# Retention and two MLPs on one core: scores as 64 by 64 products, and chunk loads into buffers that come free

## The chip, the cores and the metric

The kernel runs on one core of a Trainium2 chip. The metric is device time in microseconds (us), one launch, lower is better. TensorE (PE) multiplies and writes PSUM; its weight loads are listed apart as PEld. VectorE (DVE), ScalarE (ACT) and GpSimd (POOL) work on the products, and the queue of SyncE (SP) issues every DMA. An engine carries out its instructions in the order of the program and waits at semaphores for the others.

## The reference

```python
# retention: B=2, H=8 heads, S=768 steps, D=64
state = gamma * state + k_t (outer) v_t        # per head
y_t   = scale * q_t @ state
x = y transposed to (1536 tokens, 512)
h = x @ moe_w_in;  g = h * tanh(softplus(h));  x = g @ moe_w_out     # 512 -> 2048 -> 512
h = x @ moe2_w_in; g = h * cos(h);             out = g @ moe2_w_out
```

The weights arrive in 64-bit floats. Inputs of the large products are split into a high and a low part, and three products (high-high, high-low, low-high) are summed.

## The kernel before

The recurrence is done in chunks of 128 steps: 12 chunks, numbers 0 to 5 for the first batch entry and 6 to 11 for the second. A chunk's data (q and k transposed, v, k) are 1 MB and come by two DMAs of 512 KB (`att_load`, L281): the first half is q and k transposed ("qk"), the second v and k ("vk"). For each chunk n, TensorE does four groups of products, in this text called by their lines:

- **scores n** (L325, tile `ps_s`): for each of four pairs of heads and each head of the pair, k times q, contraction over D=64. One head's k and q lie in partitions 0 to 63, the other's in 64 to 127. The output of one product is 128 keys by 128 queries.
- **inter n** (L370, `ps_y<-qd,st`): decayed q times the state carried from chunk n-1; 64 by 64 weights. Not for chunks 0 and 6, which begin a batch entry.
- **update n** (L341, `ps_u`): k times decayed v, added to the running state. Not for chunks 5 and 11.
- **out n** (L381, `ps_y<-p,qkv`): masked scores times v.

TensorE's order is scores n+1, inter n, update n, out n, scores n+2, and so on. Beside it, DVE masks the scores (`p`, L332), ACT or POOL makes decayed v (`vd`, L305/L308), POOL makes decayed q (`qd`, L313 to L316), ACT or DVE reads the state out of PSUM (`st`, L350/L353), and ACT and DVE split the output into high and low parts (`x`, L395 and L398). After out 11 the first product of the MLPs starts (`ps_h`, L428), and from there on TensorE works on `ps_h` and `ps_o` (L451) to the end.

The order on each engine comes from a planner (`Plan`, L72): every operation is entered with a cost in us, what it needs and which buffers it takes, and a list schedule by longest remaining path then gives each engine's order. The orders of PE and of SP's first loads are given by the order of entry.

Ten of the twelve chunks have a buffer of their own: 0 and 1 in the third x tile, 2 to 4 in a pool of three, 5 to 7 in the buffers of the output weights (`wo`), 8 and 9 in those of `g`; 10 and 11 reuse the buffers of 2 and 3. So the first twenty chunk loads wait for no buffer. Each load does wait until the load eight before it has landed. SP issues the loads in this order: constants, chunks 0 to 6, the first half of the first input weights (`raw`, L211), chunks 7 to 9, the second half of these weights, chunks 10 and 11, the two halves of the next input weights.

## Time and profile before

| What | Value |
|---|---|
| Median of 3 runs | 572.69 us (571.97 to 572.76) |
| Profiled execution | 573.28 us |
| Its span on the core | 571.5 us |
| Outside the span | 1.78 us |
| PE busy in the span | 565.8 us (99%) |
| DVE, ACT, POOL busy | 382.6, 230.1, 97.5 us |
| First `ps_h` product starts | 45.7 us into the span |
| Granted PE clock, all windows | 1.00 |

The span is the time from the first to the last instruction of the core. A busy PE counts matmuls from issue to their modelled end, so consecutive ones overlap; start-to-start distances tell more than durations. One matmul of 32-bit floats stands as two records in the trace.

### The profile page before, as it was taken

How to read it: one execution, taken by the hardware profiler on the slowest of the kernel's cores; microseconds unless marked ns; L12 is line 12 of the kernel's file. 1: busy time of each engine (PE TensorE's matmuls, PEld its weight loads, DVE VectorE, ACT ScalarE, POOL GpSimd, SP SyncE). 2: the span in 40 equal slices, each digit the busy share in tenths (PEclk: the TensorE clock that was granted, in tenths of full speed). 3: DMA queues.
4: the chain of work that ended last, by engine and by line, in shares of the span. 5: the costliest groups of instructions: out<-in, count | busy, mean ns of one | idle time of the engine just before them, and what ended most of it. 6: DMA issues, size and time to landing. Idle time of an engine off the chain costs nothing.

```text
span 571.5 us, 7260 instructions
## 1 busy us (share of the span) xinstructions
PE 565.8 (99%) x3054; PEld 468.4 (82%) x3054; DVE 382.6 (67%) x416; ACT 230.1 (40%) x284; POOL 97.5 (17%) x74
## 2 busy tenths in 40 slices
PE   8999999999999999999999999999999999999997
PEld 6888888888888888888888888888888888888886
DVE  5779889662375427653487985898498894765462
ACT  3574543422303303214326465465345354354240
POOL 6680001111110301111101111032010312010000
PEclk9999999999999999999999999999999999999999
DMA  8982254422032200412021030304004010000113
GB/s 297 413 335 75 75 210 158 147 75 73 1 131 91 73 1 0 148 73 75 0 75 73 26 123 1 138 10 147 1 0 148 32 41 2 1 1 1 73 38 110
DMA packets 14721, 49.91 MB, mean 87 GB/s; under 512 B 1632, under 2 KB 2016, under 8 KB 14688
## 3 DMA queue, kind: packets, MB, share of 16 engines
q1 hardware_dynamic: 14688, 49.44, 23.4%
q8 instruction: 24, 0.39, 0.3%
q14 instruction: 9, 0.07, 0.0%
HBM read 46.29 MB, written 3.15 MB: 86 GB/s over the span
## 4 chain that ended last, share of the span: by engine, by line
PE 94%; DMA 4%; SPq 1%; ACT 0%; issue 0%; DVE 0%; ACTq 0%
PE ps_h L428 46%; PE ps_o L451 46%; DMA qkv<-qkv_dram 4%; SPq L294 1%; PE ps_y L381 1%; PE ps_y L370 1%; PE ps_s L325 1%; PE ps_u L341 0%; ACT vd L308 0%; ACT x L395 0%; DVE acc L517 0%; SPq L758 0%; ACT st L353 0%; ACTq L308 0%
## 5 line engine op out<-in xcount | busy, mean ns | idle before, releaser
L428 PE MATMUL ps_h<-x,wi 128*128 128x512 f32 x1152 | 264.8, 389 | 0.0
L428 PEld LDWEIGHTS ps_h<-x,wi 128*128 128x128 f32 x1152 | 216.1, 188 | 45.0 <-issue 0.2
L451 PE MATMUL ps_o<-wo,g 128*128 128x512 f32 (+1 forms) x588 | 132.5, 385 | 0.0
L451 PE MATMUL ps_o<-g,wo 128*128 128x512 f32 x576 | 132.3, 389 | 0.0
L451 PEld LDWEIGHTS ps_o<-wo,g 128*128 128x128 f32 x588 | 108.9, 188 | 22.1
L451 PEld LDWEIGHTS ps_o<-g,wo 128*128 128x128 f32 x576 | 108.1, 188 | 22.5
L494 DVE TENSOR_TENSOR g<-mish,g 128x1024 fp32r<-128x1024 f32 x24 | 33.4, 1393 | 59.2 <-ACT g L490 59.2
L262 POOL TENSOR_TENSOR wo<-mag,wo 128x1024 fp32r<-128x1024 f32 x14 | 35.8, 2557 | 212.8 <-ACT wo L248 212.8
L510 DVE TENSOR_TENSOR acc<-ps_o,acc 128x1024 f32<-128x1024 f32 x35 | 42.8, 1222 | 34.6 <-PE ps_o L451 34.4
L262 POOL TENSOR_TENSOR wi<-mag,wi 128x1024 fp32r<-128x1024 f32 x12 | 30.3, 2525 | 193.1 <-ACT wi L248 193.1
L461 ACT ACTIVATE mish<-ps_h 128x1024 f32<-128x1024 f32 (+1 forms) x25 | 24.9, 995 | 95.1 <-PE ps_h L428 95.1
L474 DVE SCALAR_TENSOR_TENSOR turns<-whole,turns 128x1024 f32<-128x1024 f32 x24 | 29.4, 1223 | 44.7 <-ACT whole L470 44.7
L466 ACT ACTIVATE turns<-ps_h,quarter 128x1024 f32<-128x1024 f32 x24 | 26.7, 1114 | 65.4 <-PE ps_h L428 65.1
L239 DVE SCALAR_TENSOR_TENSOR mag<-raw,mag 128x1024 uint32<-128x1024 uint32 (+1 forms) x38 | 42.2, 1110 | 1.1
L483 ACT ACTIVATE turns<-turns 128x1024 f32<-128x1024 f32 x24 | 25.5, 1062 | 34.8 <-DVE turns L480 34.6
L494 DVE TENSOR_TENSOR g<-turns,g 128x1024 fp32r<-128x1024 f32 x24 | 33.2, 1384 | 8.0 <-ACT g L490 8.0
L486 DVE TENSOR_TENSOR turns<-turns,ps_h 128x1024 f32<-128x1024 f32 x24 | 29.2, 1216 | 10.1 <-ACT turns L483 6.8
L254 DVE SCALAR_TENSOR_TENSOR mag<-raw,mag 128x1024 uint32<-128x1024 uint32 x26 | 33.7, 1301 | 0.4
L490 ACT CAST g<-turns 128x1024 fp32r<-128x1024 f32 x24 | 25.1, 1044 | 16.9 <-DVE turns L486 16.9
L248 ACT CAST wi<-mag 128x1024 fp32r<-128x1024 f32 (+1 forms) x20 | 17.5, 876 | 27.3 <-DVE mag L254 22.4
L470 ACT ACTIVATE whole<-turns,magic 128x1024 f32<-128x1024 f32 x24 | 27.7, 1153 | 0.8
L480 DVE TENSOR_SCALAR turns<-turns 128x1024 f32<-128x1024 f32 x24 | 27.0, 1126 | 0.8
(50 smaller groups left out, 330.2 us busy)
## 6 DMA issues: line engine op xcount, KB each, us to landing
qkv<-qkv_dram SPq DMA_DIRECT2D x24, 512.0 KB, 10.1
raw<-w1i_dram SPq DMA_DIRECT2D x16, 512.0 KB, 4.2
raw<-w1o_dram SPq DMA_DIRECT2D x16, 512.0 KB, 4.1
raw<-w2i_dram SPq DMA_DIRECT2D x16, 512.0 KB, 4.0
raw<-w2o_dram SPq DMA_DIRECT2D x16, 512.0 KB, 3.6
out_dram<-acc SPq DMA_DIRECT2D x11, 256.0 KB, 2.1
out_dram<-acc SPq DMA_DIRECT2D x2, 128.0 KB, 1.7
few<-consts_dram SPq DMA_DIRECT2D x1, 146.0 KB, 2.2
```

Source lines behind the costliest of these rows:

```text
L239: nc.vector.scalar_tensor_tensor(out=a, in0=high, scalar=0xC0000000, in1=a, op0=ALU.bitwise_and, op1=ALU.bitwise_or)
L254: nc.vector.scalar_tensor_tensor(out=w_all_of(it, single)[:, ns], in0=raw_t[it][:, ns, :, 0], scalar=29, in1=mag_t[it][:, ns], op0=ALU.log ...
L262: eng.tensor_sub(out=w[:, :, 1], in0=w_all_of(it, single)[:, ns].bitcast(F32), in1=w[:, :, 0].bitcast(F32))
L428: nc.tensor.matmul(h[:, 0 if h_tag(k) == "s" else f % 2, :], w[:, f % 2, a, kk * 128 : (kk + 1) * 128], x[:, b, kk, :], start=(a + b + kk ...
L451: nc.tensor.matmul(ps, lhs, rhs, start=(n == 0), stop=(n == 3 * GF - 1))
L466: nc.scalar.activation(out=t_t[k], in_=h_t[k], func=AF.Identity, scale=INV_2PI, bias=quarter)
L470: nc.scalar.activation(out=n_t[k], in_=t_t[k], func=AF.Identity, bias=magic)
L474: nc.vector.scalar_tensor_tensor(out=t, in0=n_t[k], scalar=MAGIC, in1=t, op0=ALU.subtract, op1=ALU.subtract)
L480: nc.vector.tensor_scalar(out=t, in0=t, scalar1=-0.5, scalar2=0.5, op0=ALU.max, op1=ALU.min)
L486: nc.vector.tensor_mul(out=t_t[k], in0=t_t[k], in1=h_t[k])
L494: nc.vector.tensor_sub(out=g[:, :, 1, :], in0=t_t[k], in1=g[:, :, 0, :].bitcast(F32))
L510: nc.vector.tensor_add(out=acc, in0=o_t[m * NG + G, j, p], in1=acc)
```

## The change

Scores: the 128 keys of a product are cut in two. Each group has 16 products of 64 keys by 128 queries where it had 8 of 128 by 128; for one pair of heads the four products use the four combinations of upper and lower partitions in and out. The results lie where they lay.

Buffers: a table `HOME` names one of eight places for each chunk. Chunks 5 and 6 are loaded over 0 and 1, chunks 7, 8, 9 over 2, 3, 4, chunk 11 over 7, and chunk 10 goes into one `wo` buffer. Each half has its own entry in the planner. A load into a used place waits for the last reader of that half of the earlier chunk. Chunks 10 and 11 are now entered ahead of the second half of the first weights. Two costs in the planner change.

```diff
-IN_WO = (5, 6, 7)
-IN_G = (8, 9)
+HOME = ("x0", "x1", "a0", "a1", "a2", "x0", "x1", "a0", "a1", "a2", "wo", "a0")
...
     def att_load(g, lo, hi, eng=nc.sync):
...
+        home = HOME[g]
...
+            elif home not in homes:
+                homes[home] = att_p.tile([128, 2048], F32, tag=home, name="qkv", bufs=1)
+            att[g] = homes[home]
         eng.dma_start(out=att[g][:, lo:hi], in_=qkv[g, :, lo:hi])
...
         for a in range(NPAIR):
-            for e in range(2):
-                h = slice(D * e, D * e + D)
-                nc.tensor.matmul(ss[e][:, a, :], qk[h, a, 1, :], qk[h, a, 0, :], start=True, stop=True)
+            for t in range(2):
+                keys = slice(D * t, D * t + D)
+                for e in range(2):
+                    h = slice(D * e, D * e + D)
+                    nc.tensor.matmul(
+                        ss[e][keys, a, :], qk[h, a, 1, keys], qk[h, a, 0, :], start=True, stop=True, skip_group_check=True,
+                    )
...
-        at["s", g] = op("PE", 1.05, att_scores, g, needs=at["qk", g] + [first], new=(s[1], 3, "s"), uses=[chunk(g), s[0]])
+        at["s", g] = op("PE", 0.94, att_scores, g, needs=at["qk", g] + [first], new=(s[1], 3, "s"), uses=[*chunk(g, "qk"), s[0]])
...
-            op("PE", 0.62, att_inter, g, needs=[at["st", g - 1], at["qd", g]], uses=uses, new=(("y", g), 1, y_tag(g)))
+            op("PE", 0.55, att_inter, g, needs=[at["st", g - 1], at["qd", g]], uses=uses, new=(("y", g), 1, y_tag(g)))
...
-    weight(("i", 0, 0), lambda: [chunk_loads(g, cuts) for g in (7, 8, 9)])
-    for g in (10, 11):
-        chunk_loads(g, cuts)
+    weight(("i", 0, 0), lambda: [chunk_loads(g, cuts) for g in (7, 8, 9, 10, 11)])
     weight(("i", 0, 1))
```

On PE, around the scores of chunk 1, the rows before (a row stands for so many products of one kind, with the output's shape):

```order
L787 MATMUL ps_w<-zero 128x256
L325 MATMUL ps_s<-qkv 128x128 x8
L341 MATMUL ps_u<-vd,qkv 64x64 x8
L381 MATMUL ps_y<-p,qkv 64x128 x8
L325 MATMUL ps_s<-qkv 128x128 x8
L370 MATMUL ps_y<-qd,st 64x128 x8
```

and now:

```order
L791 MATMUL ps_w<-zero 128x256
L327 MATMUL ps_s<-qkv 64x128 x16
L345 MATMUL ps_u<-vd,qkv 64x64 x8
L385 MATMUL ps_y<-p,qkv 64x128 x8
L327 MATMUL ps_s<-qkv 64x128 x16
L374 MATMUL ps_y<-qd,st 64x128 x8
```

The order of the groups on PE stays; the scores have twice as many products of half the output.

On SP, the loads from chunk 4's second half on, before, with the semaphores that each waits for (DMAHW is a DMA that landed; one row is one DMA of 512 KB):

```order
L294 DMA qkv<-qkv_dram 128x1024 [waits DMAHW2_49]
L294 DMA qkv<-qkv_dram 128x1024 [waits DMAHW3_49]
L294 DMA qkv<-qkv_dram 128x1024 [waits DMAHW4_49]
L294 DMA qkv<-qkv_dram 128x1024 [waits DMAHW5_49]
L294 DMA qkv<-qkv_dram 128x1024 [waits DMAHW6_49]
L211 DMA raw<-w1i_dram 128x1024 [waits DMAHW7_49]
L294 DMA qkv<-qkv_dram 128x1024 [waits DMAHW0_49]
L294 DMA qkv<-qkv_dram 128x1024 [waits DMAHW1_49]
L294 DMA qkv<-qkv_dram 128x1024 [waits DMAHW2_49]
L294 DMA qkv<-qkv_dram 128x1024 [waits DMAHW3_49]
```

and now:

```order
L294 DMA qkv<-qkv_dram 128x1024 [waits DMAHW2_49]
L294 DMA qkv<-qkv_dram 128x1024 [waits DMAHW3_49,PE_49]
L294 DMA qkv<-qkv_dram 128x1024 [waits DMAHW4_49,PE_49,Pool_49]
L294 DMA qkv<-qkv_dram 128x1024 [waits DMAHW5_49,Pool_49]
L294 DMA qkv<-qkv_dram 128x1024 [waits DMAHW6_49,PE_49,Activation_49]
L210 DMA raw<-w1i_dram 128x1024 [waits DMAHW7_49]
L294 DMA qkv<-qkv_dram 128x1024 [waits DMAHW0_49,Pool_49]
L294 DMA qkv<-qkv_dram 128x1024 [waits DMAHW1_49,PE_49,Activation_49]
L294 DMA qkv<-qkv_dram 128x1024 [waits DMAHW2_49,Pool_49]
L294 DMA qkv<-qkv_dram 128x1024 [waits DMAHW3_49,PE_49,Pool_49]
```

The same loads stand in the same order here; those of chunks 5 to 8 now also wait for engines that read the chunk whose place they take.

On ACT, around the decayed v of chunk 7 (`vd_499`), before. `x_467<-ps_y_474` is the high part of chunk 5's output, `st_550` the state after chunk 6, `st_603` that after chunk 7:

```order
L216 ACTIVATE mag_471<-raw_405 128x512
L308 ACTIVATE vd_499<-qkv_418,cst_92 128x64 x4
L395 CAST x_467<-ps_y_474 128x2x2x128
L308 ACTIVATE vd_499<-qkv_418,cst_92 128x64 x4
L353 ACTIVATE st_550<-ps_u_520,cst_92 128x64 x4
L395 CAST x_467<-ps_y_540 128x2x2x128
L353 ACTIVATE st_603<-ps_u_520,cst_92 128x64 x4
```

and now (`vd_573` is chunk 7's decayed v, `x_522<-ps_y_526` chunk 5's output, `st_599` the state after chunk 6):

```order
L215 ACTIVATE mag_524<-raw_463 128x512
L399 CAST x_522<-ps_y_526 128x2x2x128
L308 ACTIVATE vd_573<-qkv_188,cst_92 128x64 x4
L357 ACTIVATE st_599<-ps_u_578,cst_92 128x64 x4
L308 ACTIVATE vd_573<-qkv_188,cst_92 128x64 x4
L399 CAST x_522<-ps_y_590 128x2x2x128
L357 ACTIVATE st_666<-ps_u_578,cst_92 128x64 x4
```

The state after chunk 6 moves ahead of the second half of chunk 7's decayed v, and chunk 5's output ahead of both halves. POOL's order does not change.

## Rows read from the trace of the kernel before

**Rows 1.** The page: span; instruction queue (fetches, MB, share); chain by engine.
```profile
span 571.5 us, 7260 instructions
...
q8 instruction: 24, 0.39, 0.3%
...
PE 94%; DMA 4%; SPq 1%; ACT 0%; issue 0%; DVE 0%; ACTq 0%
```
**Rows 2.** Chain that ended last, 17 to 79 us: start us, us, what.
```profile
17.44 11.76 DMA qkv<-qkv_dram
...
29.28 0.61 ACT vd L308 x3
...
30.81 0.97 ACT vd L308 x4
...
32.07 0.99 PE ps_y L370 x16
33.06 0.62 PE ps_u L341 x16
...
45.72 32.89 PE ps_h L428 x144
```
**Rows 3.** Timeline of PE, 18.3 to 22.1 us: start us, busy us, work.
```profile
18.82 1.16 PE L325 MATMUL ps_s<-qkv 64*128 64x128 f32 x16
19.91 0.67 PE L370 MATMUL ps_y<-qd,st 64*64 64x128 f32 x16
20.51 0.69 PE L341 MATMUL ps_u<-vd,qkv 128*64 128x64 f32 x16
21.03 1.04 PE L381 MATMUL ps_y<-p,qkv 128*64 128x128 f32 x16
22.00 0.38 PE L325 MATMUL ps_s<-qkv 64*128 64x128 f32 x2
```
**Rows 4.** Line L325, its matmuls: ns min/median/max, first and last start us.
```profile
L325 PE MATMUL ps_s<-qkv x192: 272/272/373, 6.2 to 41.7; 64*128 64x128 f32 x192
```
**Rows 5.** Timeline of SP's queue, 0 to 50 us: chunk loads and weights.
```profile
16.19 8.24 SPq L294 DMA_DIRECT2D qkv<-qkv_dram  x6
25.38 0.33 SPq L211 DMA_DIRECT2D raw<-w1i_dram  x1
```
**Rows 6.** The load issued at 16.19 us (chunk 7, qk), line L294.
```profile
DMA to landing us min/median/max: 11.7/11.7/11.7
```
**Rows 7.** The load issued at 18.70 us (chunk 8, qk), line L294.
```profile
DMA to landing us min/median/max: 11.8/11.8/11.8
```
**Rows 8.** Stretches: us, busy of engines, PE clock, DMA share, GB/s.
```profile
12.40:25.20 12.80, 12.74 (x258) 10.88 (x258) 8.62 (x15) 8.42 (x31) 9.70 (x13) 1.00 1.03 415
```
**Rows 9.** Timeline of PE, 27.5 to 34 us: scores 7 and 8.
```profile
28.05 1.16 PE L325 MATMUL ps_s<-qkv 64*128 64x128 f32 x16
...
30.63 1.16 PE L325 MATMUL ps_s<-qkv 64*128 64x128 f32 x16
```
**Rows 10.** Timeline of ACT, 25 to 33 us: state after chunk 6.
```profile
31.68 0.90 ACT L353 ACTIVATE st<-ps_u,cst 128x64 f32<-128x64 f32 x4
```
**Rows 11.** Timeline of POOL, 25 to 46 us: first and last decayed q.
```profile
30.62 0.73 POOL L313 TENSOR_TENSOR qd<-qkv,cst 128x256 f32<-128x256 f32 x1 [0.18 <-DMA qkv<-qkv_dram]
31.43 1.89 POOL L316 TENSOR_TENSOR qd<-qkv,cst 64x256 f32<-64x256 f32 x2
...
41.15 1.59 POOL L316 TENSOR_TENSOR qd<-qkv,cst 64x256 f32<-64x256 f32 x2
```
**Rows 12.** Timeline, all engines, 38 to 48 us: first weights' second half; inter 11.
```profile
39.05 0.74 ACT L216 ACTIVATE mag<-raw 128x512 f32<-128x512 f32 x1
...
44.03 0.67 PE L370 MATMUL ps_y<-qd,st 64*64 64x128 f32 x16
...
45.75 0.69 DVE L239 SCALAR_TENSOR_TENSOR mag<-raw,mag 128x512 uint32<-128x512 uint32 x1
...
46.62 0.62 ACT L248 CAST wi<-mag 128x512 fp32r<-128x512 f32 x1
```

## The prediction

> **What bounds the kernel now.** First the page: the chain that ended last is TensorE for 94% and DMA for 4% [rows 1]. Then the chain in order of time: a chunk load of 17.44 us that lands at 29.20, ACT's decayed v of chunk 7 at 29.28 and its second half at 30.81, inter 7 at 32.07, and from there TensorE alone, with the first MLP product at 45.72 [rows 2]. Behind that point the chain holds no wait: all that the change can give is an earlier start of the MLPs, if their weights are ready too. So two stretches count: up to inter 7, where a load and ACT decide, and from inter 7 to 45.72, where TensorE's own groups do.

> Third, the timeline of TensorE in a chunk that waits for nothing [rows 3]: start to start scores take 1.09 us, inter 0.60, update 0.52, out 0.97, in all 3.18. To split these: a group's busy time less one matmul (272 ns, the median of scores [rows 4], which I take for all three) is the time from its first start to its last. Scores: 1.16 - 0.27 = 0.89, 16 records. Inter: 0.67 - 0.27 = 0.40, also 16. Out: 1.04 - 0.27 = 0.77. Inter's four tiles of 64 by 64 thus carry more than twice the records per us. I read out and scores as 8 rounds of two records, 0.77/7 = 0.11 us a round, and inter as 4 rounds of four, 0.40/3 = 0.13 with a longer first round. From the last start to the next group's first one it is 1.09 - 0.89 = 0.20 behind scores, 0.20 behind inter, 0.20 behind out; each time the tile shape changes.

> **The change part by part.**

> Scores. 16 products give 32 records, four at a time 8 rounds. First to last start: 7 rounds of 0.11 and a first one that is 0.07 longer, as in inter (0.40 - 2 x 0.11 = 0.18), 0.84. The step to inter keeps the tile shape, so I take one round, 0.11, for it: 0.95 against 1.09, -0.14. Inter then finds its shape set; without the long first round it takes 0.55, -0.05. Together -0.19 a chunk. Bounds: with rounds of 0.133 and a step of 0.20 still paid, 7 x 0.133 + 0.20 = 1.13, a loss of 0.04; with no long first round anywhere, 0.77 + 0.11 = 0.88 and inter 0.53, a gain of 0.28.
> [...]

> Chunks 1 to 6. Here the gain has cover: scores 7 started at 28.05 [rows 9], just as the first half of chunk 7 landed (issued 16.19, 11.7 us: 27.9 [rows 5, 6]). TensorE gets there more than a microsecond earlier and waits. Cost and gain: nothing.

> Loads. Each has 512 KB; at 415 GB/s [rows 8] that is 1.26 us, and the DMA share of 1.03 in that stretch says that the engines are full. With some nine loads' worth of time between issue and landing (11.7/1.26), a load that is issued up to some microseconds later lands in the same place of the queue, as long as the queue does not run dry. The new waits delay issues by little: chunk 5's vk half waits for out 0, chunk 6's for out 1, chunk 7's for out 2 (which before ended about 18.8, right ahead of scores 4 [rows 3], and now about 18.4, against an issue at 17.44 [rows 2]). Behind a waiting load SP holds all later ones, weights too, but five or more loads are still under way at that time. So I leave the landings of chunks 7 to 9 where they were. Chunks 10 and 11 move up by one load, since the weights' half that stood ahead of them at 25.38 [rows 5] goes behind them; nobody waited for them.

> Inter 7. Chunk 8's qk half lands at 18.70 + 11.8 = 30.5 [rows 7], and POOL and scores 8 both start then, at 30.62 and 30.63 [rows 9, 11]. That stays. Scores 8 at 30.55, inter 7 possible at 31.5. Its state: ACT's first half of the decayed v starts at 29.28 and is four pieces, as the second, which took 0.97 [rows 2]; to 30.3, then at once the state, 0.90 [rows 10], to 31.2; before, chunk 5's output and the second half stood ahead of it. So inter 7 goes at 31.5 and takes 0.55, where it began at 32.07 and spread over 0.99, being fed by the state's four parts [rows 2]. Update 7 could start at 32.05; the second half of decayed v now ends at 31.2 + 0.97 = 32.2 and holds its last quarter, about 0.1. Against 33.06 [rows 2]: -0.9.

> From there three times scores and inter follow (9 to 11): 3 x -0.19 = -0.57. Sum: -1.45.

> What is late next. POOL works from 30.62 to 41.15 + 1.59 = 42.74 with hardly a gap [rows 11], and its last piece feeds inter 11. It starts at a landing that I keep, so it ends at 42.5 to 42.7. Inter 11 would start at 44.03 [rows 12] - 1.45 = 42.6. The two meet; I take 0.1 for it. Gain 1.35, and POOL alone allows at most 44.03 - 42.6 = 1.4 unless chunk 8 lands earlier.

> Weights. The second half of the first weights goes behind four chunk loads, 4 x 1.26 = 5.0 us later: at the worst latency seen above, 25.38 + 11.8 + 5.0 = 42.2. Then ACT's magnitude 0.74 [rows 12], at most four short DVE operations of up to 0.69, and the cast of 0.62: 46.3. The product that needs it comes 12 matmuls into the MLPs, 12 x 32.89/144 = 2.74 [rows 2], at 44.4 + 2.74 = 47.1. 0.8 us to spare; cost 0.

> Sum: span 571.5 - 1.35 = 570.15; profiled execution 573.28 - 1.35 = 571.9. The median of the runs lies 0.6 below the profiled one, 572.69, so 571.3.

> **The rivals.**

> Chunks 7 and 8 land earlier. The loads land 11.7 us behind their issue though each is worth 1.26 us of transfer; if a shorter queue takes part of that lag away, TensorE runs by its own groups from chunk 4 on: from 18.82, scores 5 to 8 follow at 3.18 - 0.19 each, less the inter and update that the batch boundary lacks (0.55 and 0.52 once each): 18.82 - 0.4 + 4 x 2.99 - 1.07 = 29.3 for scores 8 in place of 30.55. That is 1.25 more: gain 2.6, 570.1. For it: DMA decides at this place. Against: the share is 1.03 either way, and a full queue in order lands the same load at the same time, however many wait behind it.

> Loads land later. If latency from issue stays, chunk 7's vk half, issued 1.0 later, lands 1.0 later: 30.2; then 0.97 and 0.90 on ACT and the hand-over, inter 7 at 32.2, update 7 at 32.9, gain 0.1 + 0.57: 572.0. More instructions are fetched as well: 12 x 16 records more, each with its weight load, 384 on 7,260 whose fetches are 24 of 0.39 MB/24 = 16 KB [rows 1]; 1.3 fetches more, each 16 KB/(415/16 GB/s) = 0.63 us of one of 16 DMA engines, 0.8 us. With all of that as lag on top it is 572.8. For it: every transfer needs all sixteen engines. Against: the queue is deep.
> [...]

> Slower: scores run two at a time. If the 64 by 64 products of one head and the two key halves don't overlap, there are 16 rounds: 1.09 + 8 x 0.11 = 1.97, +0.88 for each of 11 groups from scores 1 on. They follow one another on TensorE, so nearly all of it comes through, less some 1.5 of waits: +8, 581. It turns slower than before at about 1.2 us a group. For it: nothing. Against: inter's 16 records in 0.40 us with the same four tiles.

> **How the numbers follow.** Forecast 0.50; loads earlier 0.18; loads later 0.25; two at a time 0.04; the rest 0.03 (MLP weights late, over 1 us dearer). The forecast's own range is 1.0 to 1.7 us of gain, by POOL's end and the bounds on a chunk. About 0.2% (1.15 us) is what a measurement tells from no change. Faster: two thirds of the forecast, and the loads-earlier case, 0.51. Same: the other third and most of the late case, 0.37. Slower: 0.12. The range 570.0 to 572.9 holds the forecast, the late case and most of the early one.

> **What would show it.** Scores at 0.95 us start to start and inter at 0.55; scores 8 still at about 30.5, right at its landing; the state after chunk 6 between the halves of decayed v, update 7 near 32.1; POOL without a gap up to about 42.6; the first MLP product at 44.3 and no wait behind it. Wrong: landings of chunks 7 and 8 moved by over half a microsecond either way, a scores group at 1.1 or more, or a gap of TensorE in the first products.

## The result and the profile after

The changed kernel takes 577.49 us (median of 4 runs, 576.51 to 578.70); the kernel before, beside it on the same chip, 572.40 (4 runs, 571.97 to 572.76). The ratio is 1.009, 95% interval 1.0065 to 1.0116. The forecast was 571.3 us, range 570.0 to 572.9: wrong, and on the wrong side.

The page of after first: span, instruction queue, chain by engine.

```profile
span 574.8 us, 7648 instructions
...
q8 instruction: 25, 0.41, 0.3%
...
PE 96%; DMA 2%; issue 1%; SPq 0%; DVE 0%
```

Beside [rows 1] the span is 3.3 us longer, DMA has lost half of its share of the chain, and "issue" has come up: time in which an engine waited for nothing that the profile shows. It is 1% of the span, and more than the whole 3.3 us. The chain in order of time (start us, us, what) has it in four pieces:

```profile
19.79 0.43 PE ps_u L345 x9
20.23 0.79 issue
21.02 0.39 PE ps_u L345 x6
...
25.30 0.81 PE ps_s L327 x23
26.11 1.10 issue
27.22 0.54 PE ps_s L327 x9
...
31.74 0.80 PE ps_s L327 x20
32.54 1.44 issue
33.98 0.55 PE ps_s L327 x10
...
42.49 1.03 PE ps_s L327 x31
43.51 1.44 issue
44.96 0.27 PE ps_s L327
...
48.98 1.13 PE ps_h L432 x4
```

Each time TensorE stops in the middle of a group: update 3 behind 9 of its 16 records, scores 6 behind 23 of 32, scores 8 behind 20, scores 11 behind 31. In these four groups the waits for semaphores, on data or buffers, stand at the first two weight loads; the records behind the stops carry none, and the trace names no releaser for the idle time ahead of them. The four stops make 0.79 + 1.10 + 1.44 + 1.44 = 4.77 us of idle time. Start to start they cost more, because a stop also hides behind the modelled end of the matmul ahead of it: by PE's timeline the four stopped groups take 1.06, 1.34, 1.67 and 1.74 us longer than the same groups elsewhere, 5.8 in all. The first MLP product starts at 48.98, where it was 45.72 [rows 2].

Between the stops the groups run as forecast. PE's timeline of chunk 2 to 3 in after (start us, busy us, work), which answers to [rows 3]:

```profile
15.29 1.10 PE L327 MATMUL ps_s<-qkv 64*64 64x128 f32 x32
16.21 0.62 PE L374 MATMUL ps_y<-qd,st 64*64 64x128 f32 x16
16.76 0.69 PE L345 MATMUL ps_u<-vd,qkv 128*64 128x64 f32 x16
17.28 1.04 PE L385 MATMUL ps_y<-p,qkv 128*64 128x128 f32 x16
18.25 1.10 PE L327 MATMUL ps_s<-qkv 64*64 64x128 f32 x32
```

Start to start scores take 0.92 us, inter 0.55, update 0.52, out 0.97: 2.96 a chunk for 3.18. Those 80 matmul records come with 80 weight loads, 160 instructions a chunk; before it was 128.

Where the stops lie: all of TensorE's records, matmuls, weight loads and its semaphore instructions, are counted from the first one. The records that start behind the stops are the 705th, 961st, 1217th and 1729th; between them lie 256, 256 and 512. The instruction queue's fetches, by the page, are 0.41 MB/25 = 16 KB each, which is 64 bytes for each of 256 records; 25 times 256 is 6,400, and the page counts 6,492 matmuls and weight loads. So the stops are read here as the places where one fetched block ends and the next begins; one such boundary, at 1473, was passed without a stop. The DMA's rows of after for 24.7 to 25.9 us, just ahead of the second stop (packets, MB, share of 16 engines), show a fetch among the loads:

```profile
q1 hardware_dynamic: 131, 0.48, 98.3%
q8 instruction: 1, 0.02, 5.4%
```

### The profile page after: what moved, and what is told of

Its sections match the earlier page's. It is cut to its first block, busy times and chain, and to the rows that moved or that the text cites. A ratio compares the mean times of both kernels' runs of the same rounds, so it can differ in the third digit from the quotient of the medians.

```text
span 574.8 us, 7648 instructions
## 1 busy us (share of the span) xinstructions
PE 564.1 (98%) x3246; PEld 467.6 (81%) x3246; DVE 383.1 (67%) x416; ACT 230.3 (40%) x284; POOL 97.1 (17%) x74
## 4 chain that ended last, share of the span: by engine, by line
PE 96%; DMA 2%; issue 1%; SPq 0%; DVE 0%
PE ps_h L432 45%; PE ps_o L455 45%; PE ps_s L327 2%; PE ps_y L385 2%; DMA qkv<-qkv_dram 2%; PE ps_u L345 1%; PE ps_y L374 1%; SPq L294 0%; DVE acc L521 0%; SPq L762 0%
## 5 line engine op out<-in xcount | busy, mean ns | idle before, releaser
L514 DVE TENSOR_TENSOR acc<-ps_o,acc 128x1024 f32<-128x1024 f32 x35 | 42.7, 1221 | 34.6 <-PE ps_o L455 34.4
L261 POOL TENSOR_TENSOR wi<-mag,wi 128x1024 fp32r<-128x1024 f32 x12 | 30.3, 2527 | 192.9 <-ACT wi L247 167.2
L478 DVE SCALAR_TENSOR_TENSOR turns<-whole,turns 128x1024 f32<-128x1024 f32 x24 | 29.3, 1222 | 44.8 <-ACT whole L474 44.8
L238 DVE SCALAR_TENSOR_TENSOR mag<-raw,mag 128x1024 uint32<-128x1024 uint32 (+1 forms) x38 | 40.7, 1070 | 1.1
L490 DVE TENSOR_TENSOR turns<-turns,ps_h 128x1024 f32<-128x1024 f32 x24 | 29.1, 1214 | 10.1 <-ACT turns L487 6.8
L232 DVE TENSOR_SCALAR mag<-mag 128x1024 uint32<-128x1024 uint32 (+1 forms) x38 | 27.5, 723 | 1.1
```

The lines of the kernel that those rows point to most:

```text
L232: nc.vector.tensor_scalar(out=a, in0=a, scalar1=3, scalar2=0x3FFFFFF8, op0=ALU.logical_shift_left, op1=ALU.bitwise_and)
L238: nc.vector.scalar_tensor_tensor(out=a, in0=high, scalar=0xC0000000, in1=a, op0=ALU.bitwise_and, op1=ALU.bitwise_or)
L261: eng.tensor_sub(out=w[:, :, 1], in0=w_all_of(it, single)[:, ns].bitcast(F32), in1=w[:, :, 0].bitcast(F32))
L478: nc.vector.scalar_tensor_tensor(out=t, in0=n_t[k], scalar=MAGIC, in1=t, op0=ALU.subtract, op1=ALU.subtract)
L490: nc.vector.tensor_mul(out=t_t[k], in0=t_t[k], in1=h_t[k])
L514: nc.vector.tensor_add(out=acc, in0=o_t[m * NG + G, j, p], in1=acc)
```

## The experiments

**New scores alone**, in the buffers of before (e1), and **new buffers alone**, with the scores and costs of before (e2).

The edit of e1, against before:

```diff
-            for e in range(2):
-                h = slice(D * e, D * e + D)
-                nc.tensor.matmul(ss[e][:, a, :], qk[h, a, 1, :], qk[h, a, 0, :], start=True, stop=True)
+            for t in range(2):
+                keys = slice(D * t, D * t + D)
...
+                        ss[e][keys, a, :], qk[h, a, 1, keys], qk[h, a, 0, :], start=True, stop=True, skip_group_check=True,
...
```

The edit of e2, against after:

```diff
...
-                        ss[e][keys, a, :], qk[h, a, 1, keys], qk[h, a, 0, :], start=True, stop=True, skip_group_check=True,
...
+                nc.tensor.matmul(ss[e][:, a, :], qk[h, a, 1, :], qk[h, a, 0, :], start=True, stop=True)
...
```

> The kernel before with the 64 by 64 scores alone (and their two planner costs); buffers and order of loads as before. Theory F (fetches): TensorE runs out of instructions. The trace of the changed kernel has four gaps inside groups, 0.8 to 1.4 us, about 250 or 500 matmul and weight-load records apart, each about 1.3 us behind the end of a 16 KB instruction fetch; scores of twice the products bring 160 instead of 128 instructions a chunk. F expects gaps of the same kind here, three to five of them, 0.5 us or more each, and 574 to 577 us. Theory W (waits): the new buffer waits hold up loads and these cost the time; W expects no such gaps and 570.5 to 571.5.

> The changed kernel with the old scores (8 products of 128 by 128 and the two old planner costs); the loads go into freed buffers as changed. F: 128 instructions a chunk, a block of 256 lasts 6.4 us on TensorE, longer than the 6.1 to 6.7 us or as long as a fetch takes while loads run: no gap over 0.5 us inside a group, 571 to 573. W: the waits are all there, 575 to 578.

e1 took 577.63 us, ratio 1.0088 (1.0072 to 1.0105): all of the loss, and 0.6 us over F's range. Its PE timeline where the idle time ahead is "issue" (in brackets at the end):

```profile
21.37 0.39 PE L345 MATMUL ps_u<-vd,qkv 128*64 128x64 f32 x6 [0.79 <-issue]
27.84 0.54 PE L327 MATMUL ps_s<-qkv 64*64 64x128 f32 x9 [1.38 <-issue]
34.88 0.55 PE L327 MATMUL ps_s<-qkv 64*64 64x128 f32 x10 [1.71 <-issue]
41.07 1.09 PE L385 MATMUL ps_y<-p,qkv 128*64 128x128 f32 x15 [1.42 <-issue]
```

The first three stops come behind the same records as in after, and the boundary that after passed now has one, while after's last has none. e2 took 573.34, ratio 1.0016 (1.0006 to 1.0025), 0.3 us over F's range and well under W's. What its TensorE waited for from 12 to 46 us (us in total, times, longest us) has no "issue":

```profile
PE ps_s L325 <- DMA qkv<-qkv_dram: 0.8, 1, 0.8
PE ps_y L370 <- DVE st L350: 0.2, 1, 0.2
```

The scores make the stops; W falls.

**Loads of half the size** (e3): after, each chunk by four DMAs of 256 KB.

```diff
-    cuts = (0, 1024, 2048)
+    cuts = (0, 512, 1024, 1536, 2048)
```

> The changed kernel with each chunk loaded by four DMAs of 256 KB instead of two of 512 KB; at most eight are under way, so half as many bytes stand in the queues ahead of an instruction fetch. F: a fetch waits less for its turn (before it 3.8 us from request to its packet under load, 1.5 to 1.7 without), the gaps shrink to under 0.5 us in all or vanish, 570.5 to 573. W: the same waits for the same buffers, 576 to 578. Theory S (supply): TensorE's sequencer can't take 160 instructions in 3 us whatever the loads do: gaps as in the changed kernel, 577.

578.93 us, ratio 1.0106 (1.0085 to 1.0127), with five stops (0.65, 1.38, 0.61, 2.24, 0.54 us). F's expectation failed: they did not shrink. With seven or eight loads under way in either kernel, half the bytes were under way, and the packet came no sooner (3.2 to 4.5 us behind the start of a block, in after 3.2 to 4.4 at the four stops).

**No late loads** (e4): after without the loads of chunks 7 to 11, which compute on what lies in the places of chunks 2 to 4.

```diff
+        if g >= 7:
+            att[g] = homes[f"a{(g - 7) % 3}"]
+            return
         home = HOME[g]
```

> The changed kernel without the ten DMAs of chunks 7 to 11; these chunks compute on the data of chunks 2 to 4 that lie in the same kind of buffer (this leaves out part of the work, so its time is no version's). Instructions and their order on all engines but SP are those of the changed kernel. F: from about 22 us on, no loads stand ahead of a fetch; the gaps at 26 to 45 us vanish, the one at 20 us may stay; 569.5 to 572. S: the gaps stay, 575 or more. W: no waits for those buffers any more either, 569.5 to 572, so this run tells F and W from S, not from one another.

573.86 us, ratio 1.0021 (1.0012 to 1.0031), 1.9 us over F's and W's range and under S's. Its PE timeline has two stops and then none:

```profile
21.41 0.39 PE L348 MATMUL ps_u<-vd,qkv 128*64 128x64 f32 x6 [1.73 <-issue]
...
27.61 0.54 PE L330 MATMUL ps_s<-qkv 64*64 64x128 f32 x9 [1.10 <-issue]
```

The windows of e4 (us, busy of PE, PEld, DVE, ACT, POOL, PE clock, DMA share, GB/s), while loads run and when they have ended:

```profile
12.40:25.20 12.80, 11.06 (x286) 9.48 (x280) 7.70 (x14) 6.75 (x25) 10.05 (x14) 1.00 1.03 415
28.00:41.00 13.00, 13.00 (x345) 11.28 (x338) 10.12 (x17) 9.76 (x37) 9.49 (x12) 1.00 0.02 6
```

At a DMA share of 0.02, TensorE is busy for 13.00 of 13.00 us with the same 64 by 64 products: S falls. The second stop, which F expected to vanish, stayed: the weights' loads had moved up into the free queue, and the DMA share was still 1.04 from 25 to 26 us, when the fetch's packet came at 25.18. That stop is a part of the time over the range.

**Where the blocks end** (e9): after, with 16 more warm-up products of zeros ahead of scores 1.

```diff
-    op("PE", 1.1, zeros, 10, "u")
+    op("PE", 2.86, zeros, 26, "u")
```

> After with 16 more products of zeros (26 for 10) between scores 0 and scores 1, where TensorE waits for a load anyway; 16 products with their weight loads are 32 instructions. Theory F (the stops lie at the ends of 256-instruction blocks): every stop moves 16 matmul records earlier in the program. In after they come behind 9 of 16 records of update 3, 23 of 32 of scores 6, 20 of 32 of scores 8, 31 of 32 of scores 11; now behind 9 of 16 records of inter 3, 7 of 32 of scores 6, 4 of 32 of scores 8, 15 of 32 of scores 11 (where one falls away since its fetch came in time, another may take its place 128 records on). Time as after, 576 to 579. Rival P (the stops belong to the place: a wait for data or a buffer that the trace doesn't show): they stay at update 3, scores 6, 8 and 11 behind the same records.

576.55 us, ratio 1.0082 (1.0069 to 1.0096). Its PE timeline at the stops, each with the piece of the group ahead of it:

```profile
19.77 0.49 PE L374 MATMUL ps_y<-qd,st 64*64 64x128 f32 x9
21.44 0.45 PE L374 MATMUL ps_y<-qd,st 64*64 64x128 f32 x7 [1.18 <-issue]
...
26.27 0.44 PE L327 MATMUL ps_s<-qkv 64*64 64x128 f32 x7
27.61 0.97 PE L327 MATMUL ps_s<-qkv 64*64 64x128 f32 x25 [0.91 <-issue]
...
32.50 0.44 PE L327 MATMUL ps_s<-qkv 64*64 64x128 f32 x4
33.88 0.98 PE L327 MATMUL ps_s<-qkv 64*64 64x128 f32 x26 [0.94 <-issue]
...
42.75 0.66 PE L327 MATMUL ps_s<-qkv 64*64 64x128 f32 x15
44.48 0.70 PE L327 MATMUL ps_s<-qkv 64*64 64x128 f32 x17 [1.07 <-issue]
```

Inter 3 behind 9 of 16, scores 6 behind 7, scores 8 behind 4, scores 11 behind 15: all four stops moved, to the record, by the 16 matmuls that were put in 10 us and more ahead of them. The times would not tell this, since the stops of the two kernels begin within 0.6 us of each other. In every trace here, each stop of this kind has 192 records and a multiple of 256 ahead of it (704, 960, 1216 and 1728 in after). So in these kernels a count of instructions sets where TensorE stops, and P falls.

**New scores in some chunks**: in chunks 9 to 11 (e10) and in 0 to 8 (e11), both with the buffers of before and the costs of after. The edit of e10 against before; e11 has `g < 9`:

```diff
...
+            n = 2 if g >= 9 else 1
+            for t in range(n):
+                keys = slice(C // n * t, C // n * (t + 1))
...
```

> Before with the costs of after in the planner, and the 64 by 64 scores in chunks 9 to 11 alone. F: up to chunk 8 the instructions run as before, 256 in 6.2 to 6.5 us, and no stop is over 0.5 us; behind it at most one of 0.4, since the loads run out near 40 us. Three times 0.19 are gained: 0.6 us, less 0 to 0.7 us of stops; time 571.5 to 573.0, no difference that can be measured. Rival T (the new form of the scores itself costs, in each group): 3/12 of the loss of the kernel with new scores in all chunks, +1.3 us, 573.8.

> Before with the costs of after in the planner, and the 64 by 64 scores in chunks 0 to 8 alone: the other part. F: the stops at about 21, 28 and 35 us as in the kernel with new scores in all chunks (1.0, 1.6, 2.0 us start to start), the last smaller, since from chunk 9 on a block lasts 6.4 us again; 575 to 577. Rival T: 9/12 of the loss, +3.9 us, 576.4; the two part at the places: F has whole groups at 0.92 us and stops at three places, T a small loss in every group.

e11: 576.86 us, ratio 1.0084 (1.0070 to 1.0098), with stops at the first three places and no whole one behind chunk 8:

```profile
20.66 1.34 issue
...
27.09 1.10 issue
...
33.52 1.44 issue
...
41.02 0.08 issue
```

The places are as F had them, the sizes only roughly. e10: 573.28, ratio 1.0023 (1.0013 to 1.0033), 0.3 us over F's range. Its chain has two stops:

```profile
36.27 0.10 issue
...
40.87 0.99 issue
```

F had allowed one of 0.4. At the second the next block's packet had come 2.75 us behind the start of the block, with five loads under way then. The some 0.6 us that three chunks of faster scores were to give did not pay for the two stops. By time alone rival T (573.8 and 576.4) is as near in both kernels; what speaks against it is the place of the loss, in two stops and in four, while scores take 0.92 us between them.

**Fewer bytes under way**: each chunk by eight DMAs of 128 KB (e5); three places for all chunks (e6), four (e7), so that few loads can be issued ahead; and three places with the scores of before (e8).

The edits of e5, e6 and e7 against after; e8 is e6 with the scores and the two costs of before:

```diff
-    cuts = (0, 1024, 2048)
+    cuts = tuple(range(0, 2049, 256))
```
```diff
-HOME = ("x0", "x1", "a0", "a1", "a2", "x0", "x1", "a0", "a1", "a2", "wo", "a0")
+HOME = ("a0", "a1", "a2") * 4
```
```diff
-HOME = ("x0", "x1", "a0", "a1", "a2", "x0", "x1", "a0", "a1", "a2", "wo", "a0")
+HOME = ("x0", "x1", "a0", "a1") * 3
```

> After with every chunk loaded by eight DMAs of 128 KB instead of two of 512 KB; at most eight loads are under way, so at most 1 MB (2.5 us at 415 GB/s) stands ahead of an instruction fetch. Theory A (the fetch waits behind the bytes of the loads under way, up to some 4 us): the wait shrinks to 2.5 us or less, a block arrives within 1.0 + 1.3 us behind it, 4.8 us in all, as long as TensorE takes for a block (4.74); stops inside a group shrink to 0.3 us or vanish, time 571 to 573. Theory B (a fixed wait whenever the DMA engines are full, whatever is under way): four stops of 0.8 to 1.4 us stay, time 576 to 578.

> After with three places for all twelve chunks, so that a load can be issued only when the chunk three before it has been used; the loads stay 512 KB, but few can be under way behind the first microseconds. Theory A: behind about 20 us the fetch waits less than 2 us and no stop inside a group is left over 0.3 us; the first stop may stay, since six loads start at once. First MLP product at 44.5 to 46 us, time 571 to 573.5; what speaks against it is that a load now comes just in time, and a late load shows as a DMA wait ahead of a scores group. Theory B: a stop of 0.8 to 1.4 us every 256 instructions stays, time 576 to 578.

> As the kernel with three places, with four. Theory A: between after (eight loads under way) and three places: stops at 21 and 27 us stay in part, the later ones vanish; time 572 to 575. Theory B: as after, 576 to 578.

> Three places with the scores of before (128 by 128 products, 128 instructions a chunk) and the planner's costs of before. Both theories: no stop of over 0.5 us inside a group. It prices the three places alone: if loads come in time, it is as before (572 to 573); the difference to the kernel with three places and new scores is what the 64 by 64 products give when the fetch keeps up, by the trace of after 0.2 us a chunk, 1 to 2 us in all.

e7 came out as theory B had it; e5, e6 and e8 as neither theory did. e5: 589.83 us, ratio 1.0304 (1.0287 to 1.0321). Loads of 128 KB brought 228 GB/s (12.4 to 25.2 us) where those of 512 KB brought 415 (before and e4), and TensorE waited for chunks, not for instructions: 9.6 us for loads in 10 waits from the start to 50 us, and nothing put down to "issue". The window of e5, in the columns of e4's:

```profile
12.40:25.20 12.80, 9.84 (x214) 8.13 (x216) 5.23 (x9) 3.54 (x13) 6.58 (x9) 0.87 0.80 228
```

e6: 578.28, 1.0116 (1.0080 to 1.0151); e8: 576.58, 1.0080 (1.0059 to 1.0101): three places alone cost 4.4 us. In the trace of e8 loads come late, and behind the longest wait, 2.86 us, the granted clock was 0.50 from 32 to 35 us. e8 has no stop inside a group. What PE waited for in e8 from the start to 50 us (us in total, times, longest us):

```profile
PE ps_s L325 <- DMA qkv<-qkv_dram: 4.4, 4, 2.9
```

And three of the idle times in e6's PE timeline:

```profile
26.38 1.10 PE L327 MATMUL ps_s<-qkv 64*64 64x128 f32 x32 [1.04 <-DMA qkv<-qkv_dram]
...
40.51 1.10 PE L327 MATMUL ps_s<-qkv 64*64 64x128 f32 x32 [1.34 <-DMA qkv<-qkv_dram]
...
47.92 0.37 PE L327 MATMUL ps_s<-qkv 64*64 64x128 f32 x1 [3.35 <-issue]
```

e6 waits for loads 7 times up to 50 us, 6.2 us in all, which makes its blocks longer, and most end without a stop. The one entered at 38.10 holds such a wait too, 1.34 us, and still ends in the longest stop of all, 3.35 us, because the packet of the next came only 7.49 us behind its start. This execution is the slowest of the four of e6 (581.99 us), so the stop need not stand for the other three. e7: 577.78, 1.0101 (1.0079 to 1.0122), five stops of 0.28 to 1.63 us with four or five loads under way. So theory A, a wait in proportion to the bytes ahead, falls too; B's fixed wait is nearer, though the table shows that it is not fixed.

The fetches one by one, worked out from the times of TensorE's records, of q8's packets and of the loads (us; "enters" is the start of the first record of a block, "wait" from there to the packet of the next block, "stop" start to start of the records around its boundary):

```
kernel   enters   wait   stop   loads under way then / at the packet
before   18.29    2.52   0.10   8 / 8
before   24.54    2.91   0.06   8 / 8
after    15.57    3.20   1.02   7 / 7
after    21.02    3.80   1.37   7 / 6
after    27.21    4.42   1.71   7 / 4
after    33.98    1.72   0.05   3 / 1
after    38.48    4.12   1.71   4 / 2
e3       20.88    4.19   1.64   8 / 8  (256 KB each)
e4       27.61    1.31   0.00   2 / 0
e4       32.57    0.09   0.00   0 / 0
e5       33.97    3.44   0.00   7 / 8  (128 KB each)
e6       16.14    0.67   0.05   3 / 4
e6       38.10    7.49   3.62   4 / 4
```

A packet took about 1.0 us (0.9 to 1.6), and wherever TensorE had stopped it went on 1.2 to 1.6 us behind the packet's end. With four or more loads of 256 or 512 KB under way at the start, the wait is 2.4 to 4.5 us in all these kernels, but once 1.7 and once 7.5; with none 0.1 to 1.4; in e5, whose DMA share is 0.80 to 0.85, 0.4 to 3.4. From the start of a block to the start of the next it was 5.4 to 7.0 us wherever TensorE stopped, and 9.8 that once in e6, against the 4.7 us that a block lasts. With no load under way wait and packet took 2.7 us at most; with 1.6 behind them that makes 4.3, an estimate, since there TensorE did not stop. All this is for blocks entered ahead of the first MLP product. In the MLPs of before a block was entered at 70.28 with no load under way, the next packet came 24.5 us behind its start, and the next block began at 99.30 without a stop; so a fetch need not be asked for when a block is begun. What makes the wait, and why it is 0.67 once and 7.49 once, stays open.

No kernel beat the one before, and the experiments point to none: with the 64 by 64 scores a block lasts 4.7 us, and beside the loads it was 5.4 us or more to the next wherever TensorE stopped; and the two loads of a chunk, at 415 GB/s, take 2.5 of the 2.96 us that TensorE takes for it.

## Why the prediction was wrong, step by step

**The step that failed** is what it made of the instruction fetches. It counted the 384 new instructions rightly, as 1.3 fetches more. But its forecast put them at nothing, and only the rival with later loads priced them, as "0.63 us of one of 16 DMA engines", a lag of the loads. That TensorE itself waits for them, once in 256 instructions, was in no term and no rival. Its "-0.19 a chunk" took instructions to be at hand at any rate. Measured: four stops, 4.77 us of idle time, 5.8 start to start, more than the whole gain that was forecast. No run singles out the 0.8 us of that rival's sum as a lag of the loads: a packet took 0.89 to 1.04 us in after between 12 and 48 us, where the sum has 0.63, and chunk 8's first half landed earlier, at 29.1 for 30.5. The rows held the numbers for the question: 0.39 MB/24 = 16 KB a fetch [rows 1], 128 instructions in 3.18 us [rows 3], DMA share 1.03 [rows 8]. The trace of before also had the fetches' waits and packets (2.52 us in the table's first line, with a packet of 0.96), but not how long TensorE goes on waiting behind a packet, since no stop there shows it.

What a boundary of blocks cost differed: nothing in e4 at a DMA share of 0.02, 0.06 and 0.10 us start to start in before (table), and 0.8 to 1.4 us of idle time at four of the five boundaries from the 705th record on in after.

**Scores and inter**: right. 0.92 for 0.95 forecast, inter 0.55 for 0.55; from the last start of scores to the first of inter it is 0.09 us in after, where both have 64*64 tiles, for 0.20 in before, where the shape changes, and 0.11 was taken for it. Two products at a time, the slower rival, is refuted by the same rows: slower came, by another way.

**Landings of the loads**: forecast unmoved, and half a microsecond's move was named as a sign of being wrong. Chunk 8's first half landed 10.3 us behind its issue at 18.82, at 29.1, where before it was 30.5 [rows 7]:

```profile
DMA to landing us min/median/max: 10.3/10.3/10.3
```

But the same row stands in e10, which has the buffers of before (issue at 18.70, landing 10.3 us later). So the new buffers didn't bring it. In the traces of e1, e2, e9 and e11 chunk 8's first half landed at 28.7 to 29.5 us too, so the landing at 30.5 stands alone. The profiled execution of before lies 0.9 us over its median (573.28 for 572.40), and its slower loads are likely a part of that; the prediction took scores 7's wait for a load from that one execution. e10, with old scores up to chunk 8, ran into scores 7 without a wait:

```profile
26.21 1.09 PE L386 MATMUL ps_y<-p,qkv 128*64 128x128 f32 x16
27.23 1.16 PE L328 MATMUL ps_s<-qkv 64*128 64x128 f32 x16
```

So the cover for the gain of chunks 1 to 6 was not there in that execution. The medians differ by 5.1 us and the two profiled executions by 3.4: before's lies 0.9 over its median, after's 0.8 under its own. That before's other executions had earlier loads is argued, not seen.

What the new buffers did bring is a late issue for chunk 11's second half, 36.64 us for 30.48, behind out 7; it landed at 41.06 for 40.47, and nobody waited for it.

**Inter 7, ACT and POOL**: ACT's order came as read from the planner, the state after chunk 6 between the halves of decayed v ([rows 10] stood behind both):

```profile
29.75 1.06 ACT L308 ACTIVATE vd<-qkv,cst 128x64 f32<-128x64 f32 x4
30.98 0.93 ACT L357 ACTIVATE st<-ps_u,cst 128x64 f32<-128x64 f32 x4 [0.17 <-PE ps_u L345]
31.78 1.07 ACT L308 ACTIVATE vd<-qkv,cst 128x64 f32<-128x64 f32 x4
```

What it gives can't be told in after: the stop at 32.54 lies on top of it. POOL, named as late next, had gaps of 0.68 and 2.45 us behind 32 us; it held nobody.

**The sum**: less the idle time of the four stops the first MLP product would start at 48.98 - 4.77 = 44.2; forecast was 44.3. That agreement is luck. Less the 5.8 us that the stops cost start to start it is 43.2, near the 45.72 - 2.6 = 43.1 of the rival in which chunks 7 and 8 land earlier, and chunk 8 did land 1.3 us earlier. Both are estimates, since no run has the change without the stops. So apart from the fetches the sum of that rival, not the forecast's, fits what the trace shows. Behind that product there was no wait, as forecast. e2 shows that the new buffers alone give nothing: 1.0016, though its first MLP product came at 44.89 in its profile, the fastest of its ten runs; why its median is 0.9 us above that of before all the same stays open.

## What to carry to other kernels

Count a change in instructions as well as in work. Here TensorE executed 256 of them in 4.7 us, beside loads of 256 or 512 KB it was 5.4 to 7.0 us from block to block at the stops, and in after it stopped at the end of four blocks of five, although the chunks between took 2.96 us for 3.18. The mark of it was a stop inside a group, put down to "issue", at equal counts of records; putting a known number of instructions ahead tests it: in e9 16 more matmuls moved every stop by 16. A bound read from one execution that lies above the median of the runs may be that execution's own.

## What the chip showed that was not expected

- From the start of one block of 256 instructions to that of the next TensorE took 5.4 to 7.0 us where it stopped, with loads under way; beside idle DMA queues it ran through blocks of 4.6 to 5.0 us without a stop (e4). Halving the bytes of the loads under way did not shorten the wait for the packet (e3: 3.2 to 4.5 us, after: 3.2 to 4.4 at the stops).
- Loads of 128 KB, rows of 1 KB, ran at 228 GB/s, those of 512 KB at 416 (e5 and after, 12.4 to 25.2 us).
- In e5, where TensorE had waited 1.4 and 1.5 us for chunks at 13.5 and 15.4 us and went on waiting so, its mean granted clock was 0.87 from 12.4 to 25.2 us and 0.83 from 25.2 to 45.0; in after, with four stops of 0.8 to 1.4 us, it stayed at 1.00.
- In e6, with the stop of 3.35 us that ended at 47.92, the granted clock was 0.50 from 47 to 53 us, and inter took 1.18 us start to start for 0.55. In e8 it was 0.50 from 32 to 35 us, behind a wait of 2.86 us for a load that ended at 30.58.
